# Down and state-output steps in pairs of token tiles, as 64-row tiles of TensorE that change places halfway

One core of a Trainium2 chip. The metric is the device time of one execution in microseconds (us), the median of several. Executions more than 1.5% above the fastest of the same kernel count as slow and are left out of ratios; one of the kernel before (756.51 us) is such a one.

## The reference, cut to what matters

For 2048 tokens of width 576 the result is the sum of the input, a state-space layer and a gated feed-forward layer, both over the same layer norm:

```python
xn = _layernorm(x)
# feed-forward: D = 576, F = 4608
h = _sigmoid(xn @ w_gate) * (xn @ w_up)
y_ffn = h @ w_down
# state space: 576 complex states, a linear recurrence over the tokens
#   state[t] = Lam_bar * state[t-1] + B_bar @ xn[t];  y = 2 * Re(C @ state) + xn * Dskip
return x + y_ssm + y_ffn
```

Inputs, weights and output are bf16.

## The kernel before

The feed-forward part runs in six slots: two superblocks of 1024 tokens, times three thirds of F. Each slot computes gate and up for 12 blocks of 128 hidden features and two blocks of 512 tokens (`GateUp`), and then goes through the eight 128-token tiles of the superblock in a **down phase** (`d_step`). In the last slot of each superblock the down phase also adds the state output (`c_terms`), so a step has 21 terms there instead of 12.

Gate and up run on TensorE side by side: 576 is 9 x 64, so gate takes rows 0 to 63 of the array and up rows 64 to 127. The state input (`StateIn`, L530) does the same. A down step uses all 128 rows:

```python
# GateUp.mms: two 64-row tiles of the array, side by side
for c in range(NH):
    for gi, rows in ((0, slice(0, H)), (1, slice(H, P))):
        nc.tensor.matmul(self.ps[:, gi, cols], w[rows, c, fs], xT[self.nb][rows, c, cols], ...)

# d_step: one 128-row tile
for i in range(n):
    for a in range(2):                       # two halves of 288 output columns
        mm(pd[:, a, 0:DH], i, a)
# ... then VectorE: acc += pd, or ob = acc + pd and an output DMA (final steps)
bg.step(n * T_DTERM - 0.76 - 0.2)
```

`bg.step` queues background work on VectorE: layer norm of the next superblock, residuals, and the recurrence. Each call adds credit in us, to a cap of 5, and queues pieces as far as the credit goes. In the traces VectorE runs the pieces in the order in which the program queues them (in the changed kernel, from 264.56 to 274.07 us, it is just the order that the prediction had worked out), so where in the program a piece is queued decides what it stands behind.

Four kinds of buffer in the argument are few: four double-bank buffers in PSUM, the memory in which TensorE adds up its results, shared by all matmul groups; two each of `bure` and `buim`, into which ScalarE copies a state-input group and from which VectorE reads; two of the tag `ob`, shared by the output tiles and the scratch of the residual:

```python
def ln_resid(tt):
    tmp = lnp.tile([P, D], BF16, name="tmpxd", tag="ob", bufs=2)
    nc.vector.tensor_mul(tmp..., xns[tt], dskip_rows...)         # L270
    acc = accp.tile([P, D], FP32, name="acc", bufs=8)
    nc.vector.tensor_add(acc[:], xts[tt][:], tmp[:])             # L273

def ssm_w(nb, pt, part):                                         # L431, L432, L434/L436
    nc.vector.tensor_mul(w, t1, a[:])                            # reads bure or buim
    nc.vector.tensor_mul(tq[:], t2, b[:])                        # reads the other one
```

## Time and profile before

| | kernel before |
|---|---|
| time, fast runs | 507.01 to 507.72 us, median of all six runs 507.66 |
| profiled span | 505.7 us, granted TensorE clock (as a share of full speed) 1.000 |
| TensorE busy | 99% of the span, 98% of the chain that ended last |
| VectorE, ScalarE busy | 64%, 40% |
| down phases | six, about 177 us together |

With TensorE busy throughout, a share of busy time on another engine says nothing about the end. What counts is what TensorE does between the first matmul and the last, and whether it ever stands still. The chain of waits in order of time shows that; its lines are in the prediction.

### The profile page before, as it was taken

How to read it: one execution, taken by the hardware profiler on the slowest of the kernel's cores; microseconds unless marked ns; L12 is line 12 of the kernel's file. 1: busy time of each engine (PE TensorE's matmuls, PEld its weight loads, DVE VectorE, ACT ScalarE, POOL GpSimd, SP SyncE). 2: the span in 40 equal slices, each digit the busy share in tenths (PEclk: the TensorE clock that was granted, in tenths of full speed). 3: DMA queues.
4: the chain of work that ended last, by engine and by line, in shares of the span. 5: the costliest groups of instructions: out<-in, count | busy, mean ns of one | idle time of the engine just before them, and what ended most of it. 6: DMA issues, size and time to landing. Idle time of an engine off the chain costs nothing.

```text
span 505.7 us, 10662 instructions
## 1 busy us (share of the span) xinstructions
PE 500.9 (99%) x4536; PEld 289.6 (57%) x4536; DVE 324.6 (64%) x706; ACT 204.8 (40%) x368; POOL 90.8 (18%) x134
## 2 busy tenths in 40 slices
PE   8999999999999999999999999999999999999997
PEld 5544675444477444467764444774444774446775
DVE  5889797887888687878687768786675222222111
ACT  4955733556500756530016655005655005553000
POOL 7216320123100043110001231100431001300000
PEclk9999999999999999999999999999999999999999
DMA  8997595055220096241340652200643201600101
GB/s 207 205 183 232 134 204 89 19 147 141 49 49 25 1 180 152 68 119 58 83 95 6 160 141 49 47 25 1 162 106 86 48 25 27 184 1 1 36 25 35
DMA packets 40949, 45.59 MB, mean 90 GB/s; under 512 B 28614, under 2 KB 32326, under 8 KB 40902
## 3 DMA queue, kind: packets, MB, share of 16 engines
q0 software_dynamic: 10608, 34.22, 28.1%
q1 hardware_dynamic: 29862, 10.37, 10.6%
q8 instruction: 35, 0.57, 0.5%
q10 hardware_dynamic: 432, 0.33, 0.2%
q14 instruction: 12, 0.10, 0.1%
HBM read 34.36 MB, written 2.36 MB: 73 GB/s over the span
## 4 chain that ended last, share of the span: by engine, by line
PE 98%; DMA 1%; SPq 0%; issue 0%; DVE 0%
PE pgu L501 55%; PE pd L575 34%; PE pbu L530 7%; DMA crows<-in_A_Lambda_im_dram 1%; PE pd L583 1%; PE ptr L747 0%; PE pgu L739 0%; SPq L139 0%; SPq L192 0%; DVE ob L584 0%; PE ptr L196 0%
## 5 line engine op out<-in xcount | busy, mean ns | idle before, releaser
L501 PE MATMUL pgu<-xT,wgu 64*128 64x512 bf16 (+1 forms) x2628 | 283.7, 373 | 0.0
L501 PEld LDWEIGHTS <-wgu 64*128 64x128 bf16 x2628 | 127.7, 94 | 150.9 <-issue 0.5
L575 PE MATMUL pd<-wd,hT 128*128 128x288 bf16 x1128 | 141.4, 286 | 0.0
L507 ACT ACTIVATE sT<-pgu 128x512 bf16<-128x512 f32 x144 | 86.4, 600 | 120.8 <-PE pgu L501 119.8
L575 PEld LDWEIGHTS <-hT 128*128 128x128 bf16 x1128 | 109.9, 98 | 30.1 <-DVE hT L510 0.8
L510 DVE TENSOR_TENSOR hT<-sT,uT 128x512 bf16<-128x512 bf16 x144 | 60.6, 421 | 94.8 <-ACT uT L508 94.5
L508 ACT CAST uT<-pgu 128x512 bf16<-128x512 f32 x144 | 84.0, 583 | 0.0
L154 POOL DMA_DIRECT2D wgu<-in_B_w_gate_dram x36 | 27.6, 766 | 234.9 <-PE pgu L501 222.8
L536 ACT COPY bure<-pbu 128x512 f32<-128x512 f32 x16 | 9.4, 585 | 88.8 <-PE pbu L530 75.0
L160 POOL DMA_DIRECT2D wd<-in_B_w_down_dram x36 | 26.3, 734 | 98.6 <-PE pd L575 98.5
L595 DVE TENSOR_TENSOR acc<-acc,pd 128x576 f32<-128x576 f32 x32 | 24.0, 750 | 27.7 <-PE pd L575 27.7
L592 DVE TENSOR_TENSOR ob<-acc,pd 128x576 bf16<-128x576 f32 x15 | 11.3, 754 | 40.9 <-PE pd L575 40.9
L530 PE MATMUL pbu<-xT,bt 64*128 64x512 bf16 x288 | 33.7, 376 | 0.0
L575 PEld LDWEIGHTS <-hst 128*128 128x128 bf16 x270 | 26.4, 98 | 6.7
L154 POOL DMA_DIRECT2D wgu<-in_B_w_up_dram x36 | 26.5, 736 | 1.9 <-DMA wgu<-in_B_w_up_dram 1.9
L445 DVE TENSOR_TENSOR_SCAN gre<-r,g0re,wrim 128x512 bf16<-128x512 f32 x20 | 25.6, 1278 | 0.1
L575 PE MATMUL pd<-ctre,hst 128*128 128x288 bf16 x120 | 24.6, 286 | 0.0
L575 PE MATMUL pd<-ctim,hst 128*128 128x288 bf16 x120 | 24.6, 286 | 0.0
L530 PEld LDWEIGHTS <-bt 64*128 64x128 bf16 x288 | 13.8, 94 | 17.1 <-issue 0.7
L452 DVE TENSOR_TENSOR_SCAN gim<-r,g0im,wrim 128x512 bf16<-128x512 f32 x16 | 20.4, 1274 | 0.0
L230 DVE BATCH_NORM_STATS2 bnst<-xt 128x6 f32<-128x288 bf16 x32 | 12.5, 432 | 2.3 <-DMA xt<-in_A_x_dram 2.2
L431 DVE TENSOR_TENSOR wrim<-T,bure 128x512 bf16<-128x512 bf16 x20 | 13.7, 684 | 0.0
(119 smaller groups left out, 279.6 us busy)
## 6 DMA issues: line engine op xcount, KB each, us to landing
wgu<-in_B_w_gate_dram POOLq DMA_DIRECT2D x36, 288.0 KB, 4.2
wgu<-in_B_w_up_dram POOLq DMA_DIRECT2D x36, 288.0 KB, 4.8
wd<-in_B_w_down_dram POOLq DMA_DIRECT2D x36, 288.0 KB, 5.6
out_dram<-ob SPq DMA_DIRECT2D x15, 144.0 KB, 1.8
xt<-in_A_x_dram SPq DMA_DIRECT2D x10, 144.0 KB, 2.7
xt<-in_A_x_dram POOLq DMA_DIRECT2D x4, 144.0 KB, 7.5
bt<-ctre POOLq DMA_DIRECT2D x2, 288.0 KB, 6.4
bt<-ctim POOLq DMA_DIRECT2D x2, 288.0 KB, 7.8
```

Of the source, the lines that this page charges most:

```text
L154: eng.dma_start(w[rows, :, :], src[:, fs].rearrange("(c p) f -> p c f", p=H))
L160: nc.gpsimd.dma_start(wd[:], B_w_down[f0:f0 + FP * P, :].rearrange("(n p) d -> p n d", p=P))
L431: nc.vector.tensor_mul(w, t1, a[:])
L445: nc.vector.tensor_tensor_scan(gre[:], r_bc, w[:, 0, :], g0re[:, col], ALU.mult, ALU.add)
L452: nc.vector.tensor_tensor_scan(gim[:], r_bc, w[:, 1, :], g0im[:, col], ALU.mult, ALU.add)
L501: nc.tensor.matmul(self.ps[:, gi, cols], w[rows, c, fs], xT[self.nb][rows, c, cols], start=c == 0, stop=c == NH - 1)
L507: nc.scalar.activation(sT[:], self.ps[:, 0, :], ACT.Sigmoid)
L508: nc.scalar.copy(uT[:], self.ps[:, 1, :])
L510: nc.vector.tensor_mul(h[:], sT[:], uT[:])
L530: nc.tensor.matmul(out, w, xT[self.nb][rows, c, ts_], start=c == 0, stop=c == NH - 1)
L575: nc.tensor.matmul(out, lhsT, rhs[:, a * DH:(a + 1) * DH], start=i == 0, stop=i == n - 1)
L595: nc.vector.tensor_add(halves(acc[:]), halves(acc[:]), pd[:, :, 0:DH])
```

## The change

The intent: a change between 64-row and 128-row tiles costs TensorE something at both ends of every down phase. If the down steps run as 64-row tiles too, TensorE keeps one mode. Two token tiles are taken together: rows 0 to 63 work on the first and rows 64 to 127 on the second, and halfway they change places, so each tile gets all 128 rows of the contraction. Before each half of the second turn stands a nop (the **hold**) that depends on the last matmuls of both sides into those PSUM banks, so neither side starts in a bank before the other one has left it.

```diff
+    def d_pair(tts, terms, final):
+        n = len(terms[0])
+        pds = [ps_pair("pd") for _ in tts]
+        ends = {}
+        for turn in range(2):
+            for a in range(2):
+                if turn == 1:
+                    hold = nc.tensor.nop()
+                    for side in range(2):
+                        tc.add_manual_dep(hold.ins, ends[(side, a)].ins.name, PE_ORDER, ...)
+                for i in range(n):
+                    for side, rows in enumerate((slice(0, H), slice(H, P))):
+                        k = side ^ turn
+                        lhsT, rhs = terms[k][i]
+                        m = nc.tensor.matmul(pds[k][:, a, 0:DH], lhsT[rows, :], rhs[rows, a * DH:(a + 1) * DH],
+                                             start=turn == 0 and i == 0, stop=turn == 1 and i == n - 1)
+                        ends[(side, a)] = m
+        for tt, pd in zip(tts, pds):
+            # acc += pd, or ob = acc + pd and the output DMA
+            ...
+        for _ in tts:
+            bg.step(n * T_DTERM - 0.76 - 0.2)
...
-            for tt in range(NB_SB * TT_B):
+            for tt in range(0, NB_SB * TT_B, 2):
...
+                if slot == n_slots - 1 and tt == NB_SB * TT_B - 2:
+                    for k in range(2):
+                        d_step(tts[k], terms[k], final, last=k == 1)
+                else:
+                    d_pair(tts, terms, final)
                 if slot == 2 and final:
-                    acc_free[0] = tt + 1
+                    acc_free[0] = tt + 2
...
```

The call in `between_steps` is paired in the same way; in these runs that branch is not taken. The very last two steps stay at full height.

## The prediction

> **What bounds the kernel now.** I read the page first (busy shares, the chain that ended last), then the chain in order of time, then the timelines of ScalarE and VectorE where the down phases end. From the page:
>
> ```profile
> PE 500.9 (99%) x4536; PEld 289.6 (57%) x4536; DVE 324.6 (64%) x706; ACT 204.8 (40%) x368; POOL 90.8 (18%) x134
> ...
> PE pgu L501 55%; PE pd L575 34%; PE pbu L530 7%; DMA crows<-in_A_Lambda_im_dram 1%; PE pd L583 1%; PE ptr L747 0%; PE pgu L739 0%; SPq L139 0%; SPq L192 0%; DVE ob L584 0%; PE ptr L196 0%
> ```
>
> TensorE is 98% of the chain, so only what changes TensorE's own time changes the end. L501 (gate and up) and L530 (state input) run as two 64-row tiles side by side; L575 (down and state output) uses all 128 rows. From the chain in order of time (start, length in us, what):
>
> ```profile
> 7.99 1.11 PE pgu L739 x18
> 9.11 1.09 PE pgu L501 x18
> 10.19 1.13 PE ptr L747 x36
> ...
> 138.16 23.62 PE pd L575 x192
> 161.78 2.05 PE pbu L530 x18
> 163.83 1.94 PE pgu L501 x18
> ...
> 191.03 0.98 PE pbu L530 x18
> ...
> 219.20 41.27 PE pd L575 x336
> 260.47 2.05 PE pbu L530 x18
> 262.52 1.94 PE pgu L501 x18
> 264.46 1.94 PE pbu L530 x18
> 266.40 13.60 PE pgu L501 x126
> ```
>
> Three readings. First, two down phases of different length give the cost of one 128-row matmul of 288 columns without the phase's edges: (41.27 - 23.62) / (336 - 192) = 0.1226 us. Then 192 of them are 23.53, so entering the phase costs 23.62 - 23.53 = 0.09 us. Second, the first state-input group after a down phase takes 2.05 where others take 1.94: leaving costs 0.11. Third, a state-input group of 18 matmuls with 256 columns (the row at 191.03) takes 0.98 us, so 0.109 per side-by-side pair, and one with 512 columns 1.94 / 9 = 0.216. Both are the columns at 2.4 per ns plus 2 to 3 ns.
>
> **What the Trainium skill says.** (1) TensorEngine Tiling (Array Packing), Key Properties: changing the tiling mode, not just the tile, drains TensorE. The trace agrees: 0.09 us in, 0.11 us out, and nothing of the kind where L530 follows L501 (1.94 and 1.94). (2) TensorE: Matmul & The Clock Gate, section "Wait — 56ns, not 53.3ns?": a warm matmul of N columns takes N / 2.4 GHz plus about 2.5 ns; for 288 columns 122.5 ns, and the trace gives 122.6. The same section says the sequencer's microcode, where it decodes, spends some 62 ns on each matmul. Here it is faster: 72 matmuls, each with its own weight load, ran in 3.33 us from 7.99 on (three rows above), 46 ns each, just after a wait that had held the queue. (3) PSUM — Partial Sum Buffer, "Engine vs sequencer instructions": a nop is executed by the sequencer, not by the datapath. No run shows that yet on this engine.
>
> **The change, part by part.**
>
> *Streaming.* A pair of token tiles with n terms was 2 x 2n full matmuls, one after another: 4n x 0.1226. It becomes 8n half-height matmuls, two at a time: 4n pairs. By the third reading a pair of 288 columns takes 120 + 2.5 ns, so 0.1225. Equal: 0.0 us. Each matmul has its own weight load before and after, so loads double with the matmuls; two loads must fit in 122 ns, and two fit in 109 ns in the 256-column groups.
>
> *Mode changes.* There are six down phases. Five lose both edges. In the sixth the last two steps stay full height, so its one entry only moves. Removed: 5 x (0.09 + 0.11) = 1.0 us, all on TensorE's path.
>
> *The holds.* The pairs are 4 in each of five phases and 3 in the sixth: 23, with two holds each, 46. A hold waits for matmuls that lie n pairs back (12 x 0.1225 = 1.5 us, or 2.6 us with 21 terms); one matmul is over 0.29 us after its start (286 ns in the rows of L575). The wait is over before the array needs the next work, even if the sequencer has to pause: 0 us.
>
> *PSUM and VectorE.* Four double-bank buffers rotate. A pair takes two at its start and gives both back at its end. Inside the phase this is harmless: the pair two later needs them 5.9 or 10.3 us on. But VectorE's queue is in order, and the background work that was issued after the first step of a pair now stands behind both additions, so VectorE does nothing of it until the pair ends. At the end of a phase the work of two steps, not one, is left over. This matters only if someone waits for VectorE there. After the phases that end at 81, 162, 340 and 415 us I find no such wait that is near to TensorE: the lag of 1.5 to 3.5 us ends in idle stretches of VectorE. After the one that ends at 260.5 it matters. ScalarE's and VectorE's timelines there (start, length, instruction, idle before):
>
> ```profile
> 268.68 0.58 ACT L536 COPY bure<-pbu 128x512 f32<-128x512 f32 x1 [1.77 <-DVE tq L432]
> 269.17 0.59 ACT L537 COPY buim<-pbu 128x512 f32<-128x512 f32 x1
> ```
>
> ```profile
> 256.03 0.45 DVE L270 TENSOR_TENSOR tmpxd<-xn,dskip_rows 128x576 bf16<-128x576 bf16 x1
> ...
> 260.51 0.76 DVE L592 TENSOR_TENSOR ob<-acc,pd 128x576 bf16<-128x576 f32 x1 [0.81 <-PE pd L575]
> ...
> 267.89 0.68 DVE L432 TENSOR_TENSOR tq<-T,bure 128x512 bf16<-128x512 bf16 x1
> ```
>
> ScalarE already waits 1.77 us before it evacuates the second state-input group (264.46 to 266.40), because VectorE still reads the buffer `bure` that it must overwrite; L432 frees it at 268.57, and the evacuation is over at 269.76. Its PSUM buffer is wanted by the fourth group after it, which starts at 266.40 + 3 x 1.94 = 272.2. So there are 2.4 us of slack.
>
> Now the queue after the change. I worked out the background queue's credits by hand. A step with 21 terms gives 21 x 0.245 - 0.96 = 4.185, to a cap of 5; for the kernel before this reproduces the order of the trace. In the changed order both of the last two steps see acc_free = 6, so the third residual piece comes only after them. VectorE's order becomes: two additions (0.67 each from start to start), residuals 12 and 13 (1.28 each), h in two parts (1.13 each), first w part (1.66), residuals 14 and 15 (1.28 each), hT of the first group (0.34), then the second w part as far as L432's end (1.28). Before residual 12 one more wait: its scratch shares two buffers with `ob`, and now both hold outputs whose DMA takes 1.8 us to land. The first addition starts at 260.51 and is over at 261.27, so the buffer is free at about 263.1, where VectorE would be ready at 261.85.
>
> Sum: 263.1 + 2.56 + 2.26 + 1.66 + 2.56 + 0.34 + 1.28 = 273.8. ScalarE's two copies take 1.19: 274.95. TensorE wants the buffer at 272.2 - 0.1 = 272.1. It stands still for about 2.9 us, or 1.6 us if the DMA wait is not there. This is on the path, and nothing later gives it back.
>
> *Sum.* -1.0 + 2.9 = +1.9 us in full; the bare mode changes alone give -1.0.
>
> **The rivals.**
>
> *The intended gain, alone.* The mode changes go and VectorE's lag stays hidden: about 506.6. For it: the 2.4 us of slack, and a queue order that I worked out by hand, where one credit of 0.05 less or more moves a piece (the second w part misses the last step by 1.85 against 1.805). I give it 25 to 30%.
>
> *Holds or side changes drain TensorE.* If each of the 46 cost what a mode change costs, 0.1 us, that is +4.6 us: about 511 with or 514 with the stall too. Against it: waits on semaphores that were already met cost nothing elsewhere, since groups that begin with one keep their 1.94. 10%.
>
> *TensorE cannot be fed.* Twice as many instructions in the down phases, one per 31 ns for 23 us on end. If a matmul with its load needed 70 ns where 61 are to be had, 172 us would become 197. Against it: 46 ns at the start, though for 72 only, and one 64-row 256-column group at 54. 3 to 4%.
>
> **Range and chances.** Two outcomes are weighed: 506.6 (the gain alone) and 508 to 510.5 (the stall, with or without its DMA part). The base is the fast runs, 507.3 to 507.7; I take 507.6. Weighed: 0.28 x 506.6 + 0.62 x 509.4 + 0.1 x 512 = 508.9. A range of 506.3 to 511.2 covers the gain alone and the stall, and leaves out drained holds with the stall. Two per cent are 10 us: a gain of that size would need ten times the mode changes there are, a loss of it the fed-TensorE rival or holds twice as dear. Faster 0.01, within 2% 0.95, slower 0.04.
>
> **What would show it.** In the chain: the groups after a down phase at 1.94 instead of 2.05; phases of 192 x 0.1225 = 23.5 us as 384 matmuls (wrong, if they show 24 and more: holds or feeding). In the timeline some 12 us after the third down phase: TensorE idle for 2 to 3 us before the fourth group after the second state-input group, released by ScalarE's `buim` copy, and ScalarE in turn waiting 5 us and more for L432. VectorE waiting for an output DMA (`ob`) before L270. If the group starts without a gap there, the stall step is wrong and the time should be 506.6; if the time is lower than 506, something that I have not seen was lost at the old mode changes.

## The result, and the profile after

The changed kernel took **512.38 us** (median of six, 511.81 to 513.87) against 507.66: slower by 1.0% (ratio 1.0100, interval 1.0084 to 1.0116). A ratio here is the mean of one kernel's fast runs over the mean of the other's in the same rounds, so not quite the quotient of the medians. It lies above the predicted range, which ended at 511.2.

The chain in order of time, after the change. First the second down phase and what follows it, then the third from its start:

```profile
138.07 23.52 PE pd L616 x384
161.59 1.94 PE pbu L531 x18
...
218.90 30.89 PE pd L616 x504
...
249.81 0.77 DVE ob L623
250.60 1.74 DMA out_dram<-ob
...
260.29 1.33 DVE ob L623 x2
261.63 0.56 SPq L266
...
262.28 2.19 DMA out_dram<-ob
...
264.56 0.47 DVE tmpxd L270
...
274.16 0.61 DVE tq L432
...
275.35 0.60 ACT buim L538
...
275.99 9.63 PE pgu L502 x72
```

(L616 is the pair's matmul, L531 the state input, L502 gate and up.) The mode changes are gone: the phase takes 23.52 us where it took 23.62, and the group after it 1.94 instead of 2.05. The 384 half-height matmuls take what 192 full ones took. But in the third phase the chain leaves TensorE, for the first time in the kernel's body. It does so after three of the four pairs, at 249.8 us: VectorE adds, waits for an output DMA, and is then busy with residuals and layer norm up to the last pair's additions at 260.2. From there the chain goes through a second output DMA, VectorE again and ScalarE before it comes back to TensorE at 276.0. The timelines of TensorE, ScalarE and VectorE at that place (start, length, instruction, in brackets the idle time before it and what ended it):

```profile
265.73 5.99 PE L502 MATMUL pgu<-xT,wgu 64*128 64x512 bf16 x54
275.99 9.63 PE L502 MATMUL pgu<-xT,wgu 64*128 64x512 bf16 x72 [4.28 <-ACT buim L538]
```

```profile
274.87 0.58 ACT L537 COPY bure<-pbu 128x512 f32<-128x512 f32 x1 [8.47 <-DVE tq L432]
```

```profile
260.21 1.41 DVE L623 TENSOR_TENSOR ob<-acc,pd 128x576 bf16<-128x576 f32 x2
264.56 0.46 DVE L270 TENSOR_TENSOR tmpxd<-xn,dskip_rows 128x576 bf16<-128x576 bf16 x1 [2.95 <-DMA out_dram<-ob]
...
274.07 0.68 DVE L432 TENSOR_TENSOR tq<-T,bure 128x512 bf16<-128x512 bf16 x1
```

Followed back from the end: TensorE stands still for 4.28 us, because ScalarE has not emptied a PSUM buffer; ScalarE has waited 8.47 us (1.77 before), because VectorE still had to read `bure`; and VectorE came late to that, because both additions of the pair came at the end (x2 at 260.21), then 2.95 us for an output to land, then the work of two steps.

Also the 72 matmuls after the pause take 9.63 us, where 72 / 2 x 0.216 = 7.8 are usual. The busy table of two stretches (TensorE busy and instructions, the same for the weight loads, VectorE, ScalarE, GpSimd; then the granted TensorE clock, DMA share and GB/s):

```profile
271.70:276.00 4.30, 0.02 (x3) 0.00 (x2) 4.23 (x8) 1.13 (x3) 0.00 (x0) 1.00 0.00 0
276.67:280.08 3.41, 3.41 (x20) 1.46 (x18) 3.09 (x10) 2.86 (x7) 0.00 (x0) 0.50 0.00 0
```

In the first, TensorE does nothing for 4.3 us. In the second, which begins 0.7 us after it has resumed, the granted clock is 0.50 for 3.41 us. All six timed runs of the changed kernel show a mean clock below 1 (0.997, and 0.993 in the slowest); the kernel before has 1.000.

### The profile page after: what moved, and what is told of

The parts are those of the page before. It is cut to its first block, busy times and chain, and to the rows that moved or that the text cites. A ratio compares the mean times of both kernels' runs of the same rounds, so it can differ in the third digit from the quotient of the medians.

```text
span 510.9 us, 13370 instructions
## 1 busy us (share of the span) xinstructions
PE 502.4 (98%) x5892; PEld 312.5 (61%) x5892; DVE 322.5 (63%) x706; ACT 204.7 (40%) x368; POOL 90.8 (18%) x134
## 4 chain that ended last, share of the span: by engine, by line
PE 94%; DVE 4%; DMA 1%; ACT 0%; issue 0%; SPq 0%; ACTq 0%; DVEq 0%
PE pgu L502 54%; PE pd L616 31%; PE pbu L531 6%; DVE acc L273 1%; PE pd L576 1%; PE pd L584 1%; PE pgu L771 1%; DMA out_dram<-ob 1%; DVE tmpxd L270 1%; DVE xn L250 1%; PE ptr L779 0%; DVE ob L623 0%; ACT xT L782 0%; DVE tq L432 0%; DVE wrim L431 0%
## 5 line engine op out<-in xcount | busy, mean ns | idle before, releaser
L502 PE MATMUL pgu<-xT,wgu 64*128 64x512 bf16 (+1 forms) x2628 | 285.7, 375 | 4.3 <-ACT buim L538 4.3
L502 PEld LDWEIGHTS <-wgu 64*128 64x128 bf16 x2628 | 138.6, 94 | 146.0 <-issue 6.5
L616 PE MATMUL pd<-wd,hT 64*128 64x288 bf16 x2208 | 140.7, 283 | 0.0
L616 PEld LDWEIGHTS <-hT 64*128 64x128 bf16 x2208 | 116.3, 94 | 20.1
L511 DVE TENSOR_TENSOR hT<-sT,uT 128x512 bf16<-128x512 bf16 x144 | 60.5, 421 | 85.9 <-ACT uT L509 85.9
L626 DVE TENSOR_TENSOR acc<-acc,pd 128x576 f32<-128x576 f32 x32 | 22.7, 750 | 35.9 <-PE pd L616 35.9
L623 DVE TENSOR_TENSOR ob<-acc,pd 128x576 bf16<-128x576 f32 x14 | 9.9, 749 | 40.7 <-PE pd L616 40.7
L531 PE MATMUL pbu<-xT,bt 64*128 64x512 bf16 x288 | 33.8, 376 | 0.0
L616 PEld LDWEIGHTS <-hst 64*128 64x128 bf16 x504 | 26.4, 94 | 4.5
L616 PE MATMUL pd<-ctim,hst 64*128 64x288 bf16 x224 | 28.8, 283 | 0.0
L616 PE MATMUL pd<-ctre,hst 64*128 64x288 bf16 x224 | 28.8, 283 | 0.0
L531 PEld LDWEIGHTS <-bt 64*128 64x128 bf16 x288 | 14.6, 94 | 15.9
L432 DVE TENSOR_TENSOR tq<-T,buim 128x512 bf16<-128x512 bf16 x20 | 13.7, 684 | 0.0
```

What stands on the lines that cost most here:

```text
L511: nc.vector.tensor_mul(h[:], sT[:], uT[:])
L531: nc.tensor.matmul(out, w, xT[self.nb][rows, c, ts_], start=c == 0, stop=c == NH - 1)
L616: m = nc.tensor.matmul(pds[k][:, a, 0:DH], lhsT[rows, :], rhs[rows, a * DH:(a + 1) * DH], start=turn == 0 and i == 0, stop=turn == 1 and i ...
L626: nc.vector.tensor_add(halves(acc[:]), halves(acc[:]), pd[:, :, 0:DH])
```

## The experiments

**Theory A**: pairs do TensorE no harm. They shift VectorE's background work to the end of the phase, and after the third phase this delays the evacuation that TensorE needs, and then the clock is halved. **Rival B**: pairs cost TensorE time by themselves (holds, twice the instructions, tiles changing places). **Rival C**: the wait for the output DMA is the whole of it.

Nine kernels ran, all with correct results. e1 to e4 shared one chip and its runs of the kernel before (median 507.39); e5 to e8 were compared with those and one more (507.42), and e9 with these and one more again (507.45).

### e1: half the background work ahead of the additions

```diff
                         ends[(side, a)] = m
+        bg.step(n * T_DTERM - 0.76 - 0.2)
         for tt, pd in zip(tts, pds):
...
-        for _ in tts:
-            bg.step(n * T_DTERM - 0.76 - 0.2)
+        bg.step(n * T_DTERM - 0.76 - 0.2)
```

> One of the two steps of background work of a pair is queued ahead of the pair's two additions, so VectorE does it while TensorE works on the pair; TensorE's program is unchanged. Theory A (VectorE's leftover work at the end of the third down phase delays the buffer that the state-input group's evacuation needs): no stall of TensorE near 272 us, clock 1.000, about 506.6 us, which is 1 us under the kernel before. Rival B (pairs, holds or twice the instructions cost TensorE time by themselves): the time stays near 512.

Measured: **506.38 us** (506.17 to 506.61), clock 1.000, ratio to before 0.9981 (0.9968 to 0.9993). TensorE's and ScalarE's timelines there:

```profile
265.33 13.76 PE L502 MATMUL pgu<-xT,wgu 64*128 64x512 bf16 x126
```

```profile
267.90 0.58 ACT L537 COPY bure<-pbu 128x512 f32<-128x512 f32 x1 [1.89 <-DVE tq L432]
```

The 126 matmuls run without a pause, and ScalarE's wait is back at 1.89 us. TensorE's instructions are the same as in the changed kernel, in the same order, so rival B falls: the loss is in where VectorE's work is queued. What is left is the gain that the change was meant to have, 1.0 us. This is the lowest median; e2, next, is 0.2 us above it, and their ranges overlap.

### e2: only the third phase back to single steps

```diff
+                elif slot == 2:
+                    for k in range(2):
+                        d_step(tts[k], terms[k], final)
+                        acc_free[0] = tt + k + 1
```

> Only the third down phase goes back to single full-height steps; the other pairs stay. Theory A: no stall; four of the five removed pairs of mode changes stay removed, so 507.66 - 4 x 0.2 = about 506.9 us. Rival B: 20 of the 23 pairs less four are still there, so most of the loss stays, above 510.

Measured: **506.59 us** (506.45 to 506.69), clock 1.000, 0.80 under before. TensorE's waits show no pause there; four phases keep their gain of 0.2. So of the five phases that are wholly in pairs, only the third did harm.

### e3: the waiting group moved away

```diff
-            flush_bu()
+            if not (g.slot == NC and 1 <= i < 5):
+                flush_bu()
```

> The state-input group that has to wait is moved four gate-and-up groups later, after the third down phase; VectorE's lag is left as it is. Theory A: the waiter is gone, the stall shrinks from 4.3 us to between 0 and 1, the clock stays at 1.000, 506.6 to 507.7 us. If the lag hurts in other ways (hT buffers), a stall of more than 1 us shows up at another group. Rival B: near 512.

Measured: **507.73 us** (507.54 to 508.16). The 4.28 us pause is gone, but VectorE's lag shows up elsewhere. TensorE's and ScalarE's timelines:

```profile
287.21 8.16 PE L502 MATMUL pgu<-xT,wgu 64*128 64x512 bf16 x74 [1.01 <-ACT buim L546]
```

```profile
273.30 0.60 ACT L508 ACTIVATE sT<-pgu 128x512 bf16<-128x512 f32 x1 [4.39 <-DVE hT L511]
```

ScalarE now waits for VectorE's gate product (L511), and 14 us later TensorE pauses for 1.0 us behind the next state-input group. So taking the one waiter away is not enough; the lag itself has to go. Compared with e1 (506.38), 0.35 us beyond that pause are not accounted for. In the two profiled executions TensorE reached the third down phase 0.29 us later in e3 than in e1 (218.80 against 218.51), long before the pause, so part of it may be an uneven start.

### e4: a scratch buffer of its own for the residuals

```diff
-        tmp = lnp.tile([P, D], BF16, name="tmpxd", tag="ob", bufs=2)
+        if tt < 2 * TT_B:
+            tmp = lnp.tile([P, D], BF16, name="tmpxd", tag="ob", bufs=2)
+        else:
+            tmp = ssmp.tile([P, D], BF16, name="tmpxd", tag="ctw", bufs=1)
```

(`ctw` is a loading buffer that is dead by then.)

> The residual's scratch in the third down phase gets a buffer of its own, so it no longer waits for the output DMA of the pair; the rest as in the changed kernel. Theory A with the queue order as the larger part: VectorE is earlier by the 2.95 us wait before the last residuals, so the stall falls from 4.3 to about 1.3 us, the clock is not halved (another 1.7 us), about 507.9 us. Rival C (the DMA wait is all of it): no stall, 506.6. Rival B: near 512.

Measured: **507.81 us** (507.64 to 508.41), clock 1.000. TensorE's timeline:

```profile
272.82 7.95 PE L505 MATMUL pgu<-xT,wgu 64*128 64x512 bf16 x72 [1.40 <-ACT buim L541]
```

The pause is 1.40 us (the prediction had 1.6 without the DMA wait), and 506.38 + 1.40 = 507.78 is the time: no halved clock. Rival C falls as the sole cause: without the DMA wait the queue order alone still stalls TensorE, by a third of what it was. Both together made the pause long enough to cost the clock.

### e5: the cause without any pair

The kernel before with one thing changed: the background work of each even step is queued after the odd step's addition.

```diff
-        bg.step(n * T_DTERM - 0.76 - 0.2)
+        if late is None:
+            bg.step(n * T_DTERM - 0.76 - 0.2)
+        elif late:
+            for _ in range(2):
+                bg.step(n * T_DTERM - 0.76 - 0.2)
...
-                    acc_free[0] = tt + 1
+                    acc_free[0] = (tt + 1) // 2 * 2
```

> The kernel before, all steps at full height, but the background work of each first step is queued only after the second step's addition, as the pairs do it. TensorE's instructions are those of before. Theory A: the same wait appears without any pair. VectorE then has about 11.3 us of work from 260.5 to the read that frees the buffer (one addition fewer than with pairs, and no output DMA to wait for), so 271.8, two copies of ScalarE to 273.0, against 272.2 when TensorE wants the buffer: a stall of about 0.9 us, about 508.3 us. Rival B (the pairs themselves): no change, 507.4.

Measured: **512.52 us** (512.04 to 512.79), clock 0.997. TensorE's and VectorE's timelines:

```profile
275.36 9.63 PE L501 MATMUL pgu<-xT,wgu 64*128 64x512 bf16 x72 [3.47 <-ACT buim L537]
```

```profile
263.80 0.46 DVE L270 TENSOR_TENSOR tmpxd<-xn,dskip_rows 128x576 bf16<-128x576 bf16 x1 [2.88 <-DMA out_dram<-ob]
```

So the late background work alone, without one 64-row down step, brings the wait, the pause and the halved clock. That the time is nearly the changed kernel's is partly chance: the pause is shorter (3.47 for 4.28), and the 1.0 us of mode changes is not gained. The size that I expected (0.9 us) was wrong: I had assumed no wait for an output DMA, and it is there, 2.88 us, with the halved clock on top.

### e6: holds whose wait is not met

As e1, but the second turn takes the column halves in the order 1, 0, so each pair's first hold waits for the matmuls just issued.

```diff
-            for a in range(2):
+            for a in ((0, 1), (1, 0))[turn]:
```

> As e1_bg_between, but the second turn takes the two halves in reverse order, so in each pair the first hold waits for matmuls that have only just been issued. If a hold is free because its wait is met (my step), then here each pair shows one gap of 0.3 to 0.45 us between the turns: 23 x 0.35 = 8 us more, about 514.5. If holds were free for another reason (the wait never stops the array), the time stays at 506.4.

Measured: **511.94 us** (511.89 to 512.27), clock 1.000: 5.56 us over e1. The chain in order of time shows the breaks, where e1 has one piece for a whole phase:

```profile
59.94 6.07 PE pd L616 x96
66.06 6.07 PE pd L616 x96
```

96 matmuls take 6.12 us from start to start, instead of 96 x 0.06125 = 5.88: 0.24 us for each of the 23 waits, 5.5 together. The trace's start times agree: 23 gaps of 348 ns, one in each pair, where 122 are usual. So a hold does stop the array when its wait is not met, and the change's order (halves 0, 1, 0, 1) is what makes it free. My 0.35 was too much.

### e7: outputs on another queue

```diff
-                nc.sync.dma_start(o[tt * P:(tt + 1) * P, :], ob[:])
+                nc.scalar.dma_start(o[tt * P:(tt + 1) * P, :], ob[:])
```

> The changed kernel with the pairs' output DMAs on ScalarE's queue, so they don't stand behind the transposes on SyncE's. Tests the term that I took too small: VectorE's wait for the output DMA was 2.95 us where I had 1.25. Theory A: that wait falls by about 1 us and the chain before it by a little; TensorE's stall falls from 4.3 to about 3 us; and if the halved clock hangs on how long TensorE stands still (4.3 us did it, 1.4 didn't), it tells whether 3 us is long enough: about 509.4 us with the full clock, about 511 with 3.4 us at half.

Measured: **513.01 us** (512.09 to 513.2), clock 0.997: no better. VectorE's timeline:

```profile
263.85 0.46 DVE L270 TENSOR_TENSOR tmpxd<-xn,dskip_rows 128x576 bf16<-128x576 bf16 x1 [2.79 <-DMA out_dram<-ob]
```

TensorE's pause is 4.14 us. The DMA was issued 0.8 us after the additions began (at 260.43), where in the changed kernel it was 2.1 us (at 262.28), but it landed at 263.75, 3.3 us after its issue. So leaving SyncE's queue hardly helps: nearly all that was saved before the issue was lost after it. The transposes of the layer norm were still under way: the last one landed at about 264.8 here, at about 258.1 in the kernel before.

### e8: more mode changes

As e1, with every second pair as two full-height steps.

```diff
-                if slot == n_slots - 1 and tt == NB_SB * TT_B - 2:
+                if tt % 4 == 2:
                     for k in range(2):
                         d_step(tts[k], terms[k], final, last=...)
```

> As e1_bg_between, but every second pair is two full-height steps again, so each of the five whole phases has four mode changes (none in e1, two in the kernel before) and the sixth has three instead of one: 22 more than e1. At 0.1 us each 506.4 + 2.2 = 508.6 us, and 11 more than the kernel before, so about 1.1 us above it. If the gain of e1 came from anything else in the pairs, about half of it would be left: 506.9.

Measured: **508.78 us** (508.49 to 508.87). The second down phase in the chain (L576 is the full-height step):

```profile
137.98 5.88 PE pd L616 x96
143.87 5.99 PE pd L576 x48
149.85 5.99 PE pd L616 x96
155.84 5.99 PE pd L576 x48
161.82 2.05 PE pbu L531 x18
```

Each piece that begins with a mode change is 0.11 longer than the one that does not. 22 more changes than e1 cost 508.78 - 506.38 = 2.40 us, 0.109 each. The mode change is the whole of the change's gain.

### e9: the transposes behind the outputs

```diff
-                    add(0.0, lambda tt=tt: ln_dma_transpose(tt + TT_B))
+                    if tt < tts[2]:
+                        add(0.0, lambda tt=tt: ln_dma_transpose(tt + TT_B))
...
+                if nb == 3 and tt == tts[1]:
+                    for t in tts[2:]:
+                        add(0.0, lambda t=t: ln_dma_transpose(t))
```

> The changed kernel with the last two DMA transposes of the third down phase queued behind the last pair's output DMAs instead of ahead of them. In the changed kernel the output landed 4.1 us after its addition had begun; with the DMA issued early but the transposes still under way (e7) it landed 3.3 us after the issue. If the transposes are what holds the outputs up, VectorE's wait before the residual falls from 2.95 to about 1.4 us (issue at once, 1.8 us to land) and TensorE's stall from 4.3 to about 2.8 us, the size that I predicted: about 509.1 us if the clock stays full, 510.8 if 2.8 us are enough to halve it. If something else holds the outputs up, nothing changes: 512.4 us.

Measured: **510.51 us** (509.31 to 510.89). VectorE's and TensorE's timelines in the profiled run:

```profile
262.82 0.46 DVE L270 TENSOR_TENSOR tmpxd<-xn,dskip_rows 128x576 bf16<-128x576 bf16 x1 [1.19 <-DMA out_dram<-ob]
```

```profile
274.26 7.95 PE L502 MATMUL pgu<-xT,wgu 64*128 64x512 bf16 x72 [2.52 <-ACT buim L538]
```

The wait is 1.19 us, and the pause 2.52: the transposes were what held the outputs up, and this is near the pause that I had predicted. The clock decides the rest, and it went both ways. Two of the six runs had a clock of 1.000 and took 509.31 and 509.41 us; the other four had 0.997 and took 510.37 to 510.89. Means: 509.36 and 510.67, so the runs with the lower clock took 1.3 us longer. Only the run of 509.41 us was profiled; that the other four had the same pause is not shown.

What decides it can be seen in part. In the three traces with a halved clock (the changed kernel, e5, e7) it is at half for 3.41 us, and the full-speed stretch before it in the trace's clock record is a multiple of that (269.65 us = 79 x 3.413), as if the clock were set anew every 3.41 us. Cut along that grid, first the stretch just before the halved one in the changed kernel, then the two that hold the pause of e9:

```profile
273.25:276.67 3.42, 0.68 (x8) 0.36 (x9) 3.13 (x5) 1.80 (x4) 0.00 (x0) 1.00 0.00 0
```

```profile
269.74:273.16 3.42, 1.99 (x20) 0.78 (x15) 3.35 (x7) 0.03 (x1) 0.00 (x0) 1.00 0.00 0
273.16:276.57 3.41, 2.31 (x22) 1.24 (x23) 2.87 (x4) 3.41 (x8) 0.00 (x0) 1.00 0.00 0
```

TensorE was busy for 0.68 us of the stretch before the clock was halved (0.20 in e5 and in e7), and for 1.99 and 2.31 us of the two in e9, where the pause lies across an edge and the clock stays full. So it matters how a pause falls on the grid, and not only how long it is. Whether this is what parted the six runs of e9 is not shown.

## Why the prediction was wrong

The "within 2%" and the mechanism of the stall were right; the time was not, and the range was too low at its upper end. Two steps failed: the size of the wait for the output DMA, and the sum, which had no term for the clock. By its own steps:

- **Streaming, 0.0**: right. A phase of 384 half-height matmuls takes 23.52 us.
- **Mode changes, -1.0**: right. e1 gains 1.01 us, e8 puts 0.109 on each.
- **The holds, 0**: right, and for the reason given: e6 shows that an unmet wait costs 0.24.
- **PSUM and VectorE**: right in kind. The phase, the engine, the buffer, the instruction (L432) and the group that would wait were named, and the wait for `ob` too. Of the sum, the work between that wait and L432's end took 10.2 us where the prediction adds up 10.7.
- **"whose DMA takes 1.8 us to land", "the buffer is free at about 263.1"**: here the size failed; VectorE went on at 264.56. The 1.8 is the page's median over all outputs. I did not ask what else the DMA engines would be doing once the background work came late: the transposes came late too. VectorE's wait was 2.95 us instead of 1.25 (e9, with the transposes out of the way: 1.19), and the pause 4.28 instead of 2.9 (e9: 2.52).
- **"-1.0 + 2.9 = +1.9"**: here a term was missing. After the pause the clock is halved for 3.41 us, which costs 1.3 us (e9, from the run times) to 1.9 us (the sum below). The Trainium skill has this in TensorE: Matmul & The Clock Gate, section "What's actually happening": after an idle window of about 3.4 us the clock falls to half. I had predicted a pause of nearly that length and did not follow it up. (Here 2.74 us idle out of 3.42 were enough; see e9.)
- **The intended gain alone, at 28%**: this rival pulled the stated time below the 509.4 of the stall, to 508.9. It was wrong, as theory A's own order of the queue had said.
- **"172 us would become 197"**: a slip without effect. The six down phases in the kernel before add up to 177 us, so that rival would have given 203.

The sum, from measured terms: -1.0 (e1) + 4.28 (the pause) + 1.86 (9.63 - 7.77: 72 matmuls, some 20 of them at half the clock) = +5.1 us. The means of the fast runs differ by 512.55 - 507.47 = 5.1. Shown by runs: that the order of VectorE's queue is the cause of the pause (e1, e5), that no other phase does harm (e2), that the DMA wait is a part and not all (e4), and that the transposes cause that part (e7, e9). Not settled: how exactly the transposes slow an output, what share of a stretch must be idle to halve the clock, and e3's last 0.35 us.

## What to carry to other kernels

When steps are merged, look at what the merged step does to the engines beside it: one in-order queue that used to get work after each step gets it after every second, and its lag at the end of the phase grows (here L432 ends at 274.75 us instead of 268.57). Queue part of that work ahead of the merged step's result (e1, one line moved), and the gain stays. And a pause of TensorE should be priced with the clock that it may cost: here up to another 1.9 us after pauses of 3.5 us and more, in four runs of six where the profiled pause was 2.5 us, and in none of five at 1.4 us.

## What the Trainium skill lacked or had wrong

- TensorE: Matmul & The Clock Gate names an idle window of about 3.4 us and advises against gaps of more than about 3. Here the window need not be idle throughout: the clock was halved after a stretch of 3.42 us in which TensorE had been busy for 0.68 us. With pauses of 3.47, 4.14 and 4.28 us in the profiled run (e5, e7, the changed kernel) all timed runs had the lower clock, with 2.52 us four of six (e9), with 1.40 us none of five (e4). The half clock lasted 3.41 us, and the clock changed on a grid of that length, as the page's free-running window would have it.
- TensorEngine Tiling (Array Packing) says that a change of mode drains TensorE and gives no figure: 0.09 us in and 0.11 out here, 0.109 each over 22 more of them.
- No page that I read prices a wait between row tiles that share a PSUM bank in turn: nothing when met, 0.24 us when not (e6).
- DMA: Bandwidth & Descriptors covers DMA transposes but not their effect on plain stores issued beside them: an output tile of 144 KB landed 1.7 to 1.8 us after its issue in e9, and 3.3 us after it while transposes were under way (e7).
